# One limit and one guard per unit as sums over pairs: small softmax operations regrouped in a fused attention and gated feed-forward kernel

## The chip, the cores and the metric

One core of one Trainium2 chip. The metric is the device time of one execution in microseconds (us), given as the median of several runs. Engines are called by the profile's names: PE (TensorE, matrix products), PEld (its weight loads), DVE (VectorE), ACT (ScalarE), POOL (GpSimd) and SP (SyncE, which issues most DMAs).

## What is computed

```python
# q, k, v: (8 batches, 8 heads, 576, 64); tau = 0.02
scores = (1 / sqrt(64)) * q @ k^T
thresh = max(scores, axis=-1) - tau
scores = where(scores >= thresh, scores, -1e9)
attn = exp(scores - max(scores))
attn = attn / (sum(attn) + 1e-9)
x = (attn @ v), heads side by side                 # (8, 576, 512)

h = maximum(x @ w_in, 0)                           # w_in (512, 1024)
conv = three taps along the sequence, zero at both ends, weights (3, 1024)
out = (h * sigmoid(conv)) @ w_out                  # w_out (1024, 512)
```

All in float32. Each row of the softmax keeps only the scores within tau of the row's maximum.

## The kernel before

The work on attention is cut into 160 *units*: a pair of heads and one tile of 128 query rows, or, for the last 64 rows of a sequence, both heads in one tile of 128. For each batch the tiles form two *chunks* (rows 0 to 255 and 256 to 575), and after a chunk's units come its feed-forward products. In a unit, `unit(u, ...)`, each head goes through these steps; names in brackets are those that the profile shows:

1. PE computes the scores into a PSUM tile (`ps_s`, two buffers; L573 in batch 0, L580 after).
2. DVE takes each row's maximum with its sign turned (L588, into the small tile `few`).
3. ACT computes exp(score - maximum) into `em` (L597).
4. The *limit*, maximum minus tau, a column of 128 values, one operation for each head, on DVE, POOL or ACT (L594, L592).
5. The *mask* on DVE (L600): compare the scores with the limit, multiply with `em`, and sum the row into `few` at once.

For both heads together follow the *guard* (sum + 1e-9, L617, on DVE or POOL), its reciprocal (L624, DVE), and an operation for empty rows (L621, DVE or POOL: 1/576 where the sum is zero, else zero). Last comes the *norm* of each head, `em` x reciprocal + that column (L633, POOL in 287 of 288 cases). PE then turns `em` round (L692), ACT copies the result, and PE multiplies with v (L747, L756).

`mm1` computes one block of 128 hidden features for a chunk: PE (`ph`, L784), ReLU on ACT (L799) into `hp`, taps and gate on DVE (L806, L811), tanh on ACT (L813), and the split of the result into a high and a low part (L821 on ACT, L333 on POOL). `hp` has a column more at each end; where the chunk begins or ends a sequence POOL writes that column to zero each time (`edge`, L794 and L796). `mm2` is the last product (`po`, L842).

In the first stage DVE, POOL and ACT also split the feed-forward weights into two parts: 16 pieces of 512 columns (`stage`; L380 on POOL, L383, L386 and L389 on DVE, and L333 on POOL for four of the pieces), and 15 short DVE operations (L454) compute the ratios of the convolution's weights.

No loop sets the order in which an engine meets its operations. All steps are given to a `Plan` with a cost in nanoseconds, the tiles read and written, and other engines that may take them (`other`); a list scheduler plays through these costs and writes each engine's instructions in the order that comes out. A tile of a pool (`plan.buf`) becomes available when everything that used its buffer four (or three, two) turns before is done.

## Time and profile before

| what | value |
|---|---|
| median of 3 runs | 915.95 us (913.06 to 915.98) |
| span of the profiled execution | 910.8 us; no time of its own is given for it |
| PE busy | 874.6 us, 96% of the span |
| DVE busy | 751.2 us, 82% |
| ACT busy | 673.8 us, 74% |
| POOL busy | 603.5 us, 66% |
| L594 limits | 170 on DVE (mean 208 ns), 89 on POOL (351 ns); L592: 29 on ACT (287 ns) |
| L617 guards | 91 on POOL (296 ns), 69 on DVE (293 ns) |
| L621 empty rows | 93 on DVE (160 ns), 67 on POOL (245 ns) |
| L633 norms on POOL | 287, mean 924 ns |
| L794, L796 zero columns on POOL | 64 + 64, mean 96 and 97 ns |

The span runs from the first to the last instruction of one execution; the runs' times are some microseconds longer. A share of busy time is a mean over the whole span, in which the first stage (batch 0's attention and the weights) differs from the rest. "Idle before, releaser" in a group's row tells how long its engine waited just ahead of it, and for what.

### The profile page before, as it was taken

Reading aid. Unit: us, or ns where it says so; the run is one execution under the profiler, and the core shown is the slowest. Engines: PE = TensorE matmul, PEld = TensorE weight load, DVE = VectorE, ACT = ScalarE, POOL = GpSimd, SP = SyncE. Lnnn points to the kernel's source line nnn. Section 1 sums busy time; section 2 is a strip of 40 time slices with the busy share of each in tenths; the row PEclk is TensorE's granted clock in tenths of the full one; section 3 lists DMA queues with packets and bytes.
Section 4 is the critical chain, followed back from the end, with each engine's and each line's share of the span. In section 5 each row is a group of like instructions: output and inputs, shape, how many; then the busy total and the mean of one; then the engine's idle time right before and its main releaser. Section 6 shows DMA issues by size and latency. Waiting matters only on the chain.

```text
span 910.8 us, 19147 instructions
## 1 busy us (share of the span) xinstructions
PE 874.6 (96%) x6056; PEld 708.6 (78%) x6056; DVE 751.2 (82%) x1871; ACT 673.8 (74%) x1459; POOL 603.5 (66%) x1027
## 2 busy tenths in 40 slices
PE   5978799999999999999999999999999999999998
PEld 3545577878878788888788797887888878887896
DVE  5988999988988689987889789996988779997542
ACT  4878687878777777777768687877867778776642
POOL 2656778875767677685767767776776758675322
PEclk9989899999999999999999999999999999999999
DMA  6555257667764667647665377557667276654000
GB/s 213 155 162 170 57 143 197 149 178 181 198 175 113 163 175 198 158 116 202 169 157 157 117 201 191 140 118 202 173 176 179 89 187 159 181 137 112 13 24 35
DMA packets 148260, 137.02 MB, mean 150 GB/s; under 512 B 85312, under 2 KB 116288, under 8 KB 148160
## 3 DMA queue, kind: packets, MB, share of 16 engines
q1 hardware_dynamic: 147296, 133.90, 55.3%
q10 hardware_dynamic: 864, 1.90, 0.6%
q8 instruction: 49, 0.80, 0.4%
q14 instruction: 51, 0.42, 0.2%
HBM read 58.88 MB, written 25.95 MB: 93 GB/s over the span
## 4 chain that ended last, share of the span: by engine, by line
PE 73%; ACT 8%; DVE 6%; POOL 5%; DMA 4%; issue 3%; SPq 2%; ACTq 0%; POOLq 0%; DVEq 0%
PE po L842 20%; PE ph L784 16%; PE pa L756 12%; PE ps_s L580 11%; PE ps_t L692 9%; PE ps_s L573 3%; ACT em L597 2%; POOL em L633 2%; DVE em L600 2%; ACT eT L687 2%; PE pa L747 2%; DVE few L588 2%; DMA q<-in_qd_dram 1%; SPq L513 1%; DMA q<-q 1%
## 5 line engine op out<-in xcount | busy, mean ns | idle before, releaser
L633 POOL TENSOR_SCALAR em<-em,few 128x576 f32<-128x576 f32 x287 | 262.8, 924 | 29.9 <-DVE few L624 22.1
L600 DVE SCALAR_TENSOR_TENSOR em<-ps_s,few,em 128x576 f32<-128x576 f32 x288 | 230.5, 812 | 25.4 <-ACT em L597 17.1
L588 DVE TENSOR_REDUCE few<-ps_s 128x1 f32<-128x576 f32 x288 | 211.5, 748 | 39.3 <-PE ps_s L573 22.0
L597 ACT ACTIVATE em<-ps_s,few 128x576 f32<-128x576 f32 x288 | 210.5, 741 | 35.8 <-DVE few L588 31.5
L784 PE MATMUL ph<-x,w1h 128*128 128x322 f32 (+1 forms) x1024 | 233.7, 304 | 0.6 <-ACT hp L799 0.5
L687 ACT ACTIVATE eT<-ps_t 128x512 f32<-128x512 f32 (+2 forms) x360 | 168.0, 487 | 24.5 <-PE ps_t L692 22.4
L784 PEld LDWEIGHTS ph<-x,w1h 128*128 128x128 f32 x1024 | 173.1, 189 | 4.7 <-issue 3.0
L692 PE MATMUL ps_t<-ident,em 128*128 128x128 f32 x1060 | 157.8, 280 | 6.5 <-POOL em L633 5.1
L580 PE MATMUL ps_s<-ks,q 128*128 128x288 f32 x896 | 156.8, 306 | 5.3 <-DMA q<-q 2.1
L784 PE MATMUL ph<-x,w1l 128*128 128x322 f32 (+1 forms) x512 | 151.3, 295 | 0.0
L692 PEld LDWEIGHTS ps_t<-ident,em 128*128 128x128 f32 x1060 | 126.5, 143 | 31.5 <-POOL em L633 14.9
L580 PEld LDWEIGHTS ps_s<-ks,q 128*128 128x128 f32 x896 | 129.2, 189 | 20.2 <-issue 8.2
L333 POOL TENSOR_TENSOR gl<-t,gh 128x255 fp32r<-128x255 f32 (+9 forms) x192 | 119.6, 637 | 28.5 <-ACT gh L821 27.5
L756 PE MATMUL pa<-eT,v 128*64 128x320 f32 (+1 forms) x1024 | 132.1, 410 | 0.0
L842 PE MATMUL po<-w2h,gh 128*128 128x512 f32 x288 | 117.9, 409 | 0.3 <-ACT hp L799 0.3
L756 PEld LDWEIGHTS pa<-eT,v 128*64 128x64 f32 x1024 | 70.4, 137 | 59.3 <-issue 15.8
L842 PE MATMUL po<-w2l,gh 128*128 128x512 f32 x288 | 113.3, 393 | 0.0
L842 PE MATMUL po<-w2h,gl 128*128 128x512 f32 x288 | 113.1, 393 | 0.1
L806 DVE SCALAR_TENSOR_TENSOR t<-hp,cr 128x321 f32<-128x321 f32 (+1 forms) x128 | 75.6, 594 | 28.0 <-ACT hp L799 28.0
L784 PEld LDWEIGHTS ph<-x,w1l 128*128 128x128 f32 x512 | 96.8, 189 | 0.2
L813 ACT ACTIVATE t<-t,cm 128x321 f32<-128x321 f32 (+1 forms) x128 | 68.0, 535 | 25.2 <-DVE t L806 12.2
L811 DVE SCALAR_TENSOR_TENSOR t<-t,hp 128x321 f32<-128x321 f32 (+1 forms) x128 | 73.1, 573 | 11.4 <-ACT t L813 9.8
(80 smaller groups left out, 1104.1 us busy)
## 6 DMA issues: line engine op xcount, KB each, us to landing
q<-q SPq DMA_DIRECT2D x336, 64.0 KB, 2.1
v<-in_vc_dram SPq DMA_DIRECT2D x64, 288.0 KB, 3.8
rows<-parts SPq DMA_DIRECT2D x28, 576.0 KB, 3.3
k<-in_kp_dram SPq DMA_DIRECT2D x35, 320.0 KB, 3.5
out_dram<-ot SPq DMA_DIRECT2D x36, 256.0 KB, 2.3
xk<-in_kt_dram SPq DMA_DIRECT2D x28, 288.0 KB, 3.4
ks<-xk SPq DMA_DIRECT2D x56, 144.0 KB, 3.3
xq<-in_qt_dram SPq DMA_DIRECT2D x56, 128.0 KB, 2.9
```

Source lines behind the costliest of these rows:

```text
L333: engines[e].tensor_tensor(dst, x, y, op=ALU.subtract)
L580: nc.tensor.matmul(ps[:, c, :CH], lhsT=q[:, h, o:o + n], rhs=k[:, h, c * CH:(c + 1) * CH], start=(i == 0), stop=(i == 1))
L588: nc.vector.tensor_reduce(few[:rows, nm], ps[:rows, :, :CH], op=ALU.max, axis=mybir.AxisListType.XY, negate=True)
L597: nc.scalar.activation(view(), ps[:rows, :, :CH], AF.Exp, bias=few[:rows, nm])
L600: nc.vector.scalar_tensor_tensor(view(), ps[:rows, :, :CH], few[:rows, th], view(), op0=ALU.is_ge, op1=ALU.mult, accum_out=few[:rows, total])
L633: engines[e].tensor_scalar(sl, sl, by, to, op0=ALU.mult, op1=ALU.add)
L687: "act", act(w, True), lambda dst=dst, src=src: nc.scalar.activation(dst(), src(pt), AF.Copy),
L692: nc.tensor.transpose(out=pt[:, at:at + P], in_=em[:, int(b * P):int(b * P) + P], identity=ident[:])
L756: nc.tensor.matmul(pa[j * D:(j + 1) * D, :w], lhsT=vt[:, blk, :], rhs=eT[:, :w // D, blk, :], start=False, stop=(r == 3))
L784: nc.tensor.matmul(ph[:, :an], lhsT=w1[w][:, cb, fs], rhs=xs[cb][:, h, :an], start=(cb == 0 and i == 0), stop=(cb == NCB - 1 and i == 2))
L806: nc.vector.scalar_tensor_tensor(t[:, :kn], hp[:, k:kn + k], cr[:, j, f:f + 1], y, op0=ALU.mult, op1=ALU.add)
L842: nc.tensor.matmul(po[:], lhsT=x[:, f, at:at + P], rhs=w[:, f, :], start=(f == 0 and i == 0), stop=(f == NFB - 1 and i == 2))
```

## The change

Four small tiles `fews` and three `hps` are made once and stay; the buffers of `few` and `hp` now take them in turn (`home`) in place of pool tiles. What is constant in them is written once: tau in columns 1 and 3 of each `few`, 2^-80 x 576 in columns 5 and 7 (and in the rest until overwritten), and zero in the first and last column of each `hp`. With it:

- The limit is one operation for both heads, on DVE alone: a sum over the pairs (minus maximum, tau) with its sign turned. Both heads' masks come after it, so the first mask waits for the second head's maximum.
- The guard is a sum over the pairs (row sum, 2^-80 x 576), on DVE alone.
- There is no operation for empty rows. The norm is (em + 2^-80) x reciprocal, so that a row with no kept score comes out as 1/576. It has one per-row operand and a constant, and it may go to POOL or DVE, not to ACT.
- `edge` is gone; ReLU always writes from column 1, and the taps read from column o = 0 or 1.
- Costs in the plan differ: the norm on POOL 728 for 807, limits and guards 85, the tanh 92 more.

```diff
+    fews = [const(f"few{i}", [P, 12], F32) for i in range(FEW)]
+    hps = [const(f"hp{i}", [P, CW + 2], F32) for i in range(HPB)]
+    for x in fews:
+        op("pool", 100, lambda x=x: nc.gpsimd.memset(x[:], LEAST * S), w=[(x, 0)], ahead=200.0)
+        op(
+            "dve", 150, lambda x=x: nc.vector.tensor_scalar(x[:, 1:4:2], x[:, 1:4:2], 0.0, tau_sb[:], op0=ALU.mult, op1=ALU.add),
+            w=[(x, 0)], r=[(tau_sb, 0)], ahead=100.0
+        )
+    for x in hps:
+        op("pool", 100, lambda x=x: nc.gpsimd.memset(x[:, 0:CW + 2:CW + 1], 0.0), w=[(x, 0)], ahead=5.0)
...
-            def limit(e, nm=nm, th=th):
-                if e == "act":
-                    nc.scalar.activation(few[:rows, th], few[:rows, nm], AF.Identity, scale=-1.0, bias=ntau[:rows])
-                else:
-                    engines[e].tensor_scalar(few[:rows, th], few[:rows, nm], -1.0, ntau[:rows], op0=ALU.mult, op1=ALU.add)
+            def limit():
+                pairs = few[:rows, :2 * m].rearrange("p (h two) -> p h two", two=2)
+                nc.vector.tensor_reduce(few[:rows, 8:8 + m], pairs, negate=True, **add)
...
-            op("dve", 125, limit, w=[(few, ("th", h))], r=[(few, ("nm", h)), (ntau, 0)], ahead=a, other=[("pool", 260), ("act", 110)])
-            op("dve", 738, mask, w=[(em, h), (few, ("sum", h))], r=[(ps, 0), (few, ("th", h))], ahead=a)
+            late.append(mask)
+            if h == m - 1:
+                op("dve", 85, limit, w=[(few, "th")], r=[(few, ("nm", x)) for x in range(m)], ahead=a)
+        for h in range(m):
+            op("dve", 738, late[h], w=[(em, h), (few, ("sum", h))], r=[(pss[h], 0), (few, "th")], ahead=a)
...
-        def guard(e):
-            engines[e].tensor_scalar(few[:rows, inverse], few[:rows, sums], 1e-9, 1.0, op0=ALU.add, op1=ALU.mult)
-        def even(e):
-            engines[e].tensor_scalar(few[:rows, shift], few[:rows, sums], 0.0, 1.0 / S, op0=ALU.is_equal, op1=ALU.mult)
+        def guard():
+            pairs = few[:rows, 4:4 + 2 * m].rearrange("p (h two) -> p h two", two=2)
+            nc.vector.tensor_reduce(few[:rows, inverse], pairs, **add)
...
-                    engines[e].tensor_scalar(sl, sl, by, to, op0=ALU.mult, op1=ALU.add)
-            choice = {"pool": 807, "dve": 400, "act": 625}
+                engines[e].tensor_scalar(sl, sl, LEAST, few[:rows, 10 + h:11 + h], op0=ALU.add, op1=ALU.mult)
+            choice = {"pool": 728, "dve": 400}
...
-        def edge():
-            if o:
-                nc.gpsimd.memset(hp[:, 0:1], 0.0)
-            if k0 + kn == S:
-                nc.gpsimd.memset(hp[:, kn + 1:kn + 2], 0.0)
...
-        op("act", act(kn), lambda: nc.scalar.activation(t[:, :kn], t[:, :kn], AF.Tanh, scale=cm[:, 0, f:f + 1]), w=[(t, 0)], r=[(cr, 0)])
+        op("act", act(kn) + 92, lambda: nc.scalar.activation(t[:, :kn], t[:, :kn], AF.Tanh, scale=cm[:, 0, f:f + 1]), w=[(t, 0)], r=[(cr, 0)])
```

Since the scheduler sets the order, the whole program is ordered anew. Three places of it follow; the number at a name's end tells one use of a tile from another, and the line numbers of the changed kernel are L601 maximum, L605 limit, L611 mask, L632 guard, L635 reciprocal, L639 norm, L390 to L399 and L343 weight pieces.

First, DVE at the very start, where the first unit (`em_139` before, `em_145` now) runs. Before:

```order
L588 TENSOR_REDUCE few_132<-ps_s_0_123 128x1
L594 TENSOR_SCALAR few_132<-few_132,ntau 128x1
L588 TENSOR_REDUCE few_132<-ps_s_1_136 128x1
L600 SCALAR_TENSOR_TENSOR em_139,few_132<-ps_s_0_123,few_132,em_139 128x576
L600 SCALAR_TENSOR_TENSOR em_139,few_132<-ps_s_1_136,few_132,em_139 128x576
L588 TENSOR_REDUCE few_150<-ps_s_0_146 128x1
L624 RECIPROCAL few_132<-few_132 128x2
```

Now:

```order
L601 TENSOR_REDUCE few_77<-ps_s_0_131 128x1
L601 TENSOR_REDUCE few_77<-ps_s_1_147 128x1
L605 TENSOR_REDUCE few_77<-few_77 128x2
L611 SCALAR_TENSOR_TENSOR em_145,few_77<-ps_s_0_131,few_77,em_145 128x576
L611 SCALAR_TENSOR_TENSOR em_145,few_77<-ps_s_1_147,few_77,em_145 128x576
L601 TENSOR_REDUCE few_83<-ps_s_0_155 128x1
L632 TENSOR_REDUCE few_77<-few_77 128x2
L601 TENSOR_REDUCE few_83<-ps_s_1_159 128x1
L635 RECIPROCAL few_77<-few_77 128x2
```

The one limit stands between the second maximum and the first mask, with nothing beside it; the guard, which POOL did before, follows behind the next unit's first maximum.

Second, DVE in the second chunk of batch 0, in one unit (`em_863` before, `em_858` now) among the weight pieces. Before:

```order
L588 TENSOR_REDUCE few_849<-ps_s_0_838 128x1
L588 TENSOR_REDUCE few_849<-ps_s_1_844 128x1
L383 TENSOR_SCALAR stage_f<-stage_f 128x512
L600 SCALAR_TENSOR_TENSOR em_863,few_849<-ps_s_0_838,few_849,em_863 128x576
L386 SCALAR_TENSOR_TENSOR stage_f<-stage_712,stage_f 128x512
L600 SCALAR_TENSOR_TENSOR em_863,few_849<-ps_s_1_844,few_849,em_863 128x576
L389 SCALAR_TENSOR_TENSOR stage_f<-stage_712,stage_f 128x512
L621 TENSOR_SCALAR few_849<-few_849 128x2
L588 TENSOR_REDUCE few_900<-ps_s_0_883 128x1
```

Now:

```order
L601 TENSOR_REDUCE few_83<-ps_s_0_811 128x1
L601 TENSOR_REDUCE few_83<-ps_s_1_818 128x1
L605 TENSOR_REDUCE few_83<-few_83 128x2
L611 SCALAR_TENSOR_TENSOR em_858,few_83<-ps_s_0_811,few_83,em_858 128x576
L393 TENSOR_SCALAR stage_f<-stage_f 128x512
L611 SCALAR_TENSOR_TENSOR em_858,few_83<-ps_s_1_818,few_83,em_858 128x576
L396 SCALAR_TENSOR_TENSOR stage_f<-stage_763,stage_f 128x512
L632 TENSOR_REDUCE few_83<-few_83 128x2
L393 TENSOR_SCALAR stage_f<-stage_f 128x512
```

Both limits were POOL's here; the one that takes their place stands in DVE's line.

Third, POOL in the same stretch, with that unit's norm and the next one's. Before:

```order
L594 TENSOR_SCALAR few_849<-few_849,ntau 128x1 x2
L617 TENSOR_SCALAR few_849<-few_849 128x2
L380 TENSOR_SCALAR stage_f<-stage_f 128x512
L594 TENSOR_SCALAR few_900<-few_900,ntau 128x1
L633 TENSOR_SCALAR em_863<-em_863,few_849 128x576 x2
L594 TENSOR_SCALAR few_900<-few_900,ntau 128x1
L380 TENSOR_SCALAR stage_f<-stage_f 128x512
L617 TENSOR_SCALAR few_900<-few_900 128x2
L333 TENSOR_TENSOR w2l<-stage_f,w2h 128x512
L380 TENSOR_SCALAR stage_f<-stage_f 128x512
L633 TENSOR_SCALAR em_906<-em_906,few_900 128x576 x2
```

Now:

```order
L390 TENSOR_SCALAR stage_f<-stage_f 128x512 x2
L639 TENSOR_SCALAR em_858<-em_858,few_83 128x576
L343 TENSOR_TENSOR w2l<-stage_f,w2h 128x512
L639 TENSOR_SCALAR em_858<-em_858,few_83 128x576
L390 TENSOR_SCALAR stage_f<-stage_f 128x512
L343 TENSOR_TENSOR w2l<-stage_f,w2h 128x512
L390 TENSOR_SCALAR stage_f<-stage_f 128x512
L343 TENSOR_TENSOR w2l<-stage_f,w2h 128x512
L343 TENSOR_TENSOR gl<-t_0_929,gh 128x255
L639 TENSOR_SCALAR em_969<-em_969,few_85 128x576 x2
```

The four limits and two guards are gone from POOL's line; a unit's two norms now have a weight piece between them, and the next unit's come behind three of the four pieces that POOL subtracts.

More of the change, by code (lines that the diff above doesn't have):

```diff
@@ L21 @@
 HUGE = 3.0e38
+LEAST = 2.0 ** -80
+FEW = 4
 AHEAD = {'s': 6.25, 's4': 7.75, 't': 3.5, 'a': 3.5, 'prep': 4.25, 'w': 2.5, 'load': 7.75}
@@ L63, in __init__ @@
         self.pool, self.tag, self.bufs, self.shape, self.dtype, self.name = pool, tag, bufs, shape, dtype, name
-        self.tile, self.left = None, 0
+        self.tile, self.left, self.home = None, 0, None
     def __getitem__(self, key):
         if self.tile is None:
-            self.tile = self.pool.tile(self.shape, self.dtype, tag=self.tag, bufs=self.bufs, name=self.name)
+            self.tile = self.home or self.pool.tile(self.shape, self.dtype, tag=self.tag, bufs=self.bufs, name=self.name)
         return self.tile[key]
@@ L312, in tile_tau_attention_gated_ffn @@
     op("act", 450, lambda: nc.scalar.dma_start(tau_sb[:], tau.broadcast_to([P, 1])), w=[(tau_sb, 0)], ahead=205.0, late=2500)
-    ntau = const("ntau", [P, 1], F32)
-    op("dve", 70, lambda: nc.vector.tensor_scalar(ntau[:], tau_sb[:], -1.0, None, op0=ALU.mult), w=[(ntau, 0)], r=[(tau_sb, 0)], ahead=6.0)
+    fews = [const(f"few{i}", [P, 12], F32) for i in range(FEW)]
[8 more added lines that the diff above has]
+        op("pool", 100, lambda x=x: nc.gpsimd.memset(x[:, 0:CW + 2:CW + 1], 0.0), w=[(x, 0)], ahead=5.0)
     warm = const("warm", [P, 1], F32)
@@ L558, in unit @@
         em = plan.buf(wk, "em", EMS, [P, 2 * S], F32, f"em_{u}")
-        few = plan.buf(sm, "few", 4, [P, 10], F32, f"few_{u}")
+        few = plan.buf(sm, "few", FEW, [P, 12], F32, f"few_{u}")
+        few.home = fews[few.turn % FEW]
         a = AHEAD["s" if 2 * n > P else "s4"]
-        tiny = [("pool", 200)]
+        late, pss = [], []
+        add = dict(op=ALU.add, axis=mybir.AxisListType.X)
         for h, js in enumerate(heads):
             ps = plan.buf(ps_s, "ps_s", 2, [P, 2, 512], F32, f"ps_s_{u}_{h}")
-            nm, th, total = (slice(at + h, at + h + 1) for at in (0, 2, 4))
+            pss.append(ps)
+            nm, th, total = (slice(at, at + 1) for at in (2 * h, 8 + h, 4 + 2 * h))
             def mm(h=h, js=js, ps=ps):
@@ L608, in unit @@
             )
[L609 removed]
+            op("dve", 668, top, w=[(few, ("nm", h))], r=[(ps, 0), (few.home, 0)], ahead=a)
             op("act", 625, exp, w=[(em, h)], r=[(ps, 0), (few, ("nm", h))], ahead=a)
[L611 to L623 removed]
+            late.append(mask)
[3 more added lines that the diff above has]
+            op("dve", 738, late[h], w=[(em, h), (few, ("sum", h))], r=[(pss[h], 0), (few, "th")], ahead=a)
+        ss = [(few, ("sum", h)) for h in range(m)]
+        inverse = slice(10, 10 + m)
+        def guard():
+            pairs = few[:rows, 4:4 + 2 * m].rearrange("p (h two) -> p h two", two=2)
+            nc.vector.tensor_reduce(few[:rows, inverse], pairs, **add)
+        op("dve", 85, guard, w=[(few, "inverse")], r=ss, ahead=a)
         op("dve", 82, lambda: nc.vector.reciprocal(few[:rows, inverse], few[:rows, inverse]), w=[(few, "inverse")], ahead=a)
[L625 removed]
         for h in range(m):
@@ L638, in unit @@
             op(
-                home, choice[home], norm, w=[(em, h)], r=[(few, "inverse"), (few, "shift")], ahead=a, port=True,
+                home, choice[home], norm, w=[(em, h)], r=[(few, "inverse")], ahead=a, port=True,
                 other=[(e, ns) for e, ns in choice.items() if e != home]
```

24 lines of the change are left out of this document (8 added, 16 removed).

## The prediction

> **What bounds the kernel now.** I read the busy time of each engine stage by stage first (TensorE, PE, is busy 96% of the span on the page, which hides the difference between the stages), then what PE waits for, then the chain of work through the slow stretch, and last the prices of the small operations.
>
> ```profile
> 0.00:114.00 114.00, 90.43 (x518) 53.24 (x518) 94.14 (x225) 82.08 (x166) 65.67 (x108) 0.94 0.48 151
> 114.00:800.00 686.00, 677.23 (x4858) 565.09 (x4856) 592.74 (x1497) 531.86 (x1158) 491.19 (x828) 1.00 0.63 164
> ```
>
> The columns are the stretch, its length, then busy time of PE, PEld, DVE, ACT and POOL, granted clock, DMA share and GB/s. From 114 us on PE is the bound: 98.7% busy to 800 us, idle for 686.0 - 677.2 = 8.8 us. An operation taken off DVE, ACT or POOL there can be worth no more than that idle time. The first 114 us are another stage: PE is idle for 114.0 - 90.4 = 23.6 us, and DVE is the fullest engine (94.1 us, though its first limit starts only at 8.6). So the change is judged by the start. What PE waits for there, and the four stretches of 10 us that hold its two longest stalls (columns as before):
>
> ```profile
> PE ps_s L573 <- DVE em L600: 9.0, 4, 4.6
> PE ps_s L573 <- ACT q L503: 6.4, 1, 6.4
> PE ps_t L692 <- POOL em L633: 3.8, 6, 1.2
> PE ps_s L573 <- issue: 2.9, 1, 2.9
> ```
>
> ```profile
> 40.00:50.00 10.00, 7.35 (x49) 4.28 (x49) 8.74 (x32) 6.50 (x14) 4.21 (x9) 1.00 0.61 191
> 50.00:60.00 10.00, 7.86 (x26) 4.49 (x26) 7.99 (x20) 6.90 (x13) 4.41 (x7) 0.66 0.38 117
> ...
> 100.00:110.00 10.00, 5.07 (x36) 2.80 (x36) 9.91 (x22) 6.75 (x13) 6.11 (x9) 0.79 0.27 76
> 110.00:120.00 10.00, 9.99 (x63) 6.55 (x63) 8.81 (x24) 8.21 (x20) 6.53 (x12) 0.87 0.28 69
> ```
>
> The 6.4 us is the first load; no edit touches it. The 9.0 us are waits for a mask (L600), whose end frees a score tile. They and the 2.9 us lie mostly in two stalls: one of 4.6 us that ends at 52 us, where DVE computes the convolution's ratios, and one in two pieces, 2.0 and 2.9 us, between 101 and 108 us, where DVE is busy 9.91 of 10 us. After each the granted clock falls, to a mean of 0.66 in one stretch, and of 0.79 and 0.87 in two.
>
> **The change part by part.** First, POOL. Through the start the chain of work steps onto POOL's small operations seven times (0.19 to 0.79 us each); the list by line, the first with the crossing behind it, and the last three are:
>
> ```profile
> by line: issue 12.0%; DVE em L600 11.2%; PE ps_s L573 9.6%; POOL em L633 9.6%; DVE few L588 9.2%; ACT eT L687 4.2%; ACT em L597 4.2%; DVE stage_f L386 4.2%; PE ps_t L692 4.0%; DMA q<-in_qd_dram 3.8%; POOL stage_f L380 3.6%; DVE stage_f L389
> ...
> 65.54 0.56 POOL few L617
> 66.10 0.08 issue
> ...
> 86.56 0.42 POOL few L594
> ...
> 89.10 0.79 POOL few L594
> ...
> 90.83 0.30 POOL few L617
> ```
>
> All seven add up to 2.7 us. The changed kernel has no limit, guard or empty-row operation on POOL (its list there shows norms, weight pieces and the large subtractions alone), so I count -2.7, and -0.5 for seven crossings of some 0.08 us, since what takes their place stands in DVE's own line. Bounds: nothing, if another engine is as late at each of these places, and the whole that leaves POOL in the start, fifteen limits and fifteen guards by their medians, 15 x 0.265 + 15 x 0.301 = 8.5 us:
>
> ```profile
> L594 POOL TENSOR_SCALAR few<-few,ntau x15: 258/265/789, 9.8 to 89.1; 128x1 f32<-128x1 f32 x15
> L594 DVE TENSOR_SCALAR few<-few,ntau x11: 195/202/215, 8.6 to 110.7; 128x1 f32<-128x1 f32 x11
> L617 POOL TENSOR_SCALAR few<-few x15: 191/301/569, 11.5 to 113.2; 128x2 f32<-128x2 f32 x12, 128x1 f32<-128x1 f32 x3
> L617 DVE TENSOR_SCALAR few<-few x3: 142/155/169, 16.0 to 70.2; 128x2 f32<-128x2 f32 x2, 128x1 f32<-128x1 f32 x1
> L621 DVE TENSOR_SCALAR few<-few x13: 139/161/165, 16.1 to 113.4; 128x2 f32<-128x2 f32 x11, 128x1 f32<-128x1 f32 x2
> L624 DVE RECIPROCAL few<-few x18: 153/159/168, 12.7 to 113.8; 128x2 f32<-128x2 f32 x14, 128x1 f32<-128x1 f32 x4
> ```
>
> Second, the norm. It keeps its engine and size and exchanges one of two per-row operands for a number. No row has that form; the nearest are the norm itself and a POOL operation with two numbers on 512 columns:
>
> ```profile
> L633 POOL TENSOR_SCALAR em<-em,few x30: 816/827/1499, 13.0 to 109.5; 128x576 f32<-128x576 f32 x30
> L380 POOL TENSOR_SCALAR stage_f<-stage_f x16: 612/612/1006, 14.6 to 99.2; 128x512 f32<-128x512 f32 x16
> ```
>
> At 576 columns the second would be 612 x 576 / 512 = 689 ns. With one operand of each kind I take the middle, 758 ns, or 0.07 us less. The chain's list by line gives POOL's norm 9.6% of the start, 10.9 us or 13 norms, which makes -0.9 (bounds 0 and 13 x 0.138 = -1.8). In the steady part the same 0.07 us times 257 shortens an engine on which PE hardly waits.
>
> Third, what DVE takes over. Eighteen units (L624's count) lie in the start; their 18 limits, 18 guards and 18 reciprocals make 54 small operations, where DVE had 11 + 3 + 13 + 18 = 45 (six limits were on ACT). A row's duration isn't what it costs in DVE's line:
>
> ```profile
> 16.04 0.15 DVE L617 TENSOR_SCALAR few<-few 128x2 f32<-128x2 f32 x1
> 16.11 0.15 DVE L621 TENSOR_SCALAR few<-few 128x2 f32<-128x2 f32 x1
> 16.23 0.17 DVE L624 RECIPROCAL few<-few 128x2 f32<-128x2 f32 x1
> ```
>
> ```profile
> 306.80 1.42 DVE L588 TENSOR_REDUCE few<-ps_s 128x1 f32<-128x576 f32 x2 [3.83 <-PE ps_s L573]
> 308.26 0.21 DVE L594 TENSOR_SCALAR few<-few,ntau 128x1 f32<-128x1 f32 x1
> 308.44 0.82 DVE L600 SCALAR_TENSOR_TENSOR em<-ps_s,few,em 128x576 f32<-128x576 f32 x1
> ```
>
> Starts are 0.07 to 0.12 us apart where operations follow freely; I take 0.11. Where a limit stands directly between the maximum it needs and the mask that needs it, the step costs 0.30: two maxima that follow each other take 2 x 0.67 of the 1.64 us from the first's start to the mask's. A sum over pairs has no row; it is DVE work on two or four elements, nearest to the reciprocal of two, so I price it the same way. In the changed order 4 of the first 18 limits stand so, against two places before; the others have a weight piece or a reciprocal beside them. That makes 9 x 0.11 + 2 x 0.19 = +1.4. Bounds: all 18 limits at 0.30 and nothing cheaper elsewhere, 18 x 0.30 + 36 x 0.11 - (2 x 0.30 + 43 x 0.11) = +4.0; and, if every new one costs 0.07 and every old one 0.12, 54 x 0.07 - 45 x 0.12 = -1.6.
>
> Fourth, one limit for two heads: the first mask now waits for the second maximum, and the score tile behind it, with the next scores on PE, for that mask. In the order before, 118 of the 128 two-head units already run both maxima ahead of the first mask. Of the ten others four lie in the start, so at most 4 x 0.67 = 2.7 us, and nothing where DVE fills the time with weight pieces. I take +0.5.
>
> Fifth, DVE's weight operations stretch while POOL works on long ones:
>
> ```profile
> L389 DVE SCALAR_TENSOR_TENSOR stage_f<-stage,stage_f 128x512 uint32<-128x512 uint32 x16 | 13.8, 864 | 0.0
> ```
>
> ```profile
> L389 DVE SCALAR_TENSOR_TENSOR stage_f<-stage,stage_f x16: 674/690/1757, 23.2 to 103.5; 128x512 uint32<-128x512 uint32 x16
> ```
>
> The median is 0.690 us and the longest 1.757; the sixteen average 0.864, so 16 x 0.174 = 2.8 us of DVE's start go there. POOL's busy time in the start falls by the 8.5 us above and 30 x 0.07, a sixth of 65.7. I take the same share of the 2.8, -0.5 (bounds 0 and -2.8). [...]
>
> Sixth, the zero columns. The memsets (0.10 us each, 128 of them, six in the start) leave POOL's queue, where they waited for a tile that DVE still read and held the norms behind them. In the start POOL's chain holds none of them: 0. Seven small memsets and four setup operations on tau come ahead of the first maximum; the 6.4 us in which PE waits for its first load cover them.
>
> Seventh, the steady part. Of its 8.8 us of idle PE these name POOL's norm or DVE's softmax:
>
> ```profile
> PE ps_t L692 <- POOL em L633: 1.3, 3, 0.7
> PE ps_s L580 <- DVE em L600: 1.1, 2, 0.6
> PE ps_s L580 <- DVE few L594: 1.0, 2, 0.7
> ```
>
> That is 3.4 us; the order is planned anew and some waits return in other places, so I take a third, -1.2 (bounds -3.4, and +2 if as many new ones appear). PE's own work is the same list of products; the changes between kinds of products number 524 before and 526 after, counted in the order, and cost the same.
>
> The sum: -2.7 - 0.5 - 0.9 + 1.4 + 0.5 - 0.5 + 0 - 1.2 = -3.9 us. The span of 910.8 becomes 906.9. No separate time is given for the profiled execution; two of the three runs lie at 915.95 and 915.98, 5.15 us above the span, the third at 913.06, 2.3 above. I keep the median's distance: 912.0 us. The three runs differ by 0.3%, about what a measurement of this kernel can tell from no change, so 0.3% (2.7 us) is the bound of "same": 913.2 to 918.7.
>
> **The rivals.** One: the second stall goes as a whole. Behind its 4.9 us of idle PE the clock is missing 10 x 0.21 + 10 x 0.13 = 3.4 us of full speed. If the masks at 102 us come three microseconds earlier, PE has no gap long enough to lose its clock: -4.9 - 3.4 - 1.2 gives 906.4. For it: the chain from 86 to 100 us runs mostly over POOL, which loses 0.42 + 0.79 + 0.30 us of small work there. Against it: the four weight pieces that POOL subtracts itself remain, and DVE was without a gap. [...] Here the clock fell after two waits of 2.0 and 2.9 us.
>
> Two: nothing measurable. DVE paces the start and POOL's freed time is covered by it at each of the seven places. Then only +1.4 + 0.5 - 1.2 remain: 916.7. For it: DVE's work in the start doesn't shrink, and its limits and guards there were mostly on POOL already. Against it: POOL's pieces do stand in the chain.
>
> Three: slower. The new sums are dearer than a small operation, because each waits for its predecessor on DVE's own pipeline: at 0.30 for every limit the third term is +4.0, and at 0.30 for every guard too (18 x 0.19 more) +7.4. With DVE the pacer and nothing gained from POOL, +4.0 gives 920.0; it decides (over 918.7) from 0.23 us a limit on. For it: DVE is busy 94 of the 114 us, with its first limit at 8.6. Against it: 14 of the 18 limits have other work beside them. [...]
>
> **How the numbers follow.** The forecast (909 to 913.2) gets 0.36, the vanished stall (under 909) 0.20, no difference 0.27, slower 0.17. Faster is the sum of the first two, 0.56. The range leaves out the slower case and little of the low end: 904 (the stall's 906.4 less the steady part's other 2.2) to 918.7. The forecast's own range is 909 to 913.2: below it half of the room between 2.7 and 8.5 us of POOL, above it what reads as no difference.
>
> **What would show it.** In the changed profile: no POOL group on few apart from four memsets, and some 100 us less busy time there; a norm between 0.69 and 0.83 us; 160 limits and 160 guards on DVE with starts near 0.11 apart; PE idle of about 20 us in the first 114, and under 9 from there to 800. The stall at 48 us should remain, the one at 102 us should be shorter. The prediction is wrong if DVE's small operations hold it at over 0.2 us each, if the re-planned order opens a stall of its own after 114 us, or if the second stall's half clock vanishes.

## The result: 0.56% slower

| kernel | median of the runs, us | ratio to before, 95% interval |
|---|---|---|
| before | 915.81 (913.06 to 915.98) | |
| changed | 920.09 (918.24 to 921.62) | 1.0056 [1.0039, 1.0073] |

The forecast was 912.0, faster, in a range of 904 to 918.7. The time lies above the range, and at the number of rival three (920.0).

The profiled execution of the changed kernel has a span of 918.3 us in a time of 920.09, 1.8 us around the span, and in all runs on record it is 1.7 to 2.0. So the 910.8 us of the profile of before belong to a time of some 912.6 us (an estimate, 910.8 + 1.8), below all runs of the table, and not to the median. First the two stretches that the prediction set out from, of the changed kernel (columns as there):

```profile
0.00:114.00 114.00, 88.80 (x512) 53.16 (x513) 93.97 (x235) 78.61 (x155) 52.34 (x75) 0.95 0.46 151
114.00:800.00 686.00, 676.37 (x4807) 559.88 (x4807) 581.39 (x1459) 526.08 (x1127) 404.34 (x525) 1.00 0.64 164
```

PE did 88.8 us of work in the first 114 where it did 90.4 before: the start became worse by 1.6 us. In the second stretch it idles for 9.6 us, before 8.8. POOL lost what was foreseen (the page has 502.0 us for 603.5), and no engine is fuller than it was. The last of the start and what comes right behind it, in stretches of 10 us:

```profile
90.00:100.00 10.00, 8.04 (x53) 5.56 (x51) 8.09 (x15) 6.58 (x14) 7.35 (x8) 0.91 0.01 2
100.00:110.00 10.00, 6.50 (x48) 3.52 (x44) 7.95 (x20) 4.91 (x10) 5.35 (x6) 0.84 0.26 75
110.00:120.00 10.00, 7.63 (x39) 6.40 (x39) 7.83 (x19) 6.34 (x14) 5.69 (x7) 0.73 0.35 83
120.00:130.00 10.00, 9.18 (x51) 5.32 (x52) 8.16 (x20) 6.10 (x15) 4.05 (x5) 0.83 0.24 70
```

Before, PE was busy for 10.00, 5.07 and 9.99 of the 10 us in the first three of these rows. Now it has three stalls in four stretches (94 to 98, 104 to 110 and 116 to 122 us), with the granted clock below 1 from 90 to 130, and DVE isn't full in any of them. PE's longest waits from 90 to 126 us name ACT:

```profile
PE pa L753 <- ACT eT L693: 4.5, 3, 2.5
PE ph L791 <- ACT hp L800: 2.5, 1, 2.5
PE ps_s L586 <- DVE em L611: 0.7, 1, 0.7
```

Where the first of the three begins shows on POOL:

```profile
89.05 1.94 POOL L639 TENSOR_SCALAR em<-em,few 128x576 f32<-128x576 f32 x1 [1.79 <-DVE few L635]
90.96 1.28 POOL L343 TENSOR_TENSOR w2l<-stage_f,w2h 128x512 fp32r<-128x512 f32 x1
92.23 0.75 POOL L639 TENSOR_SCALAR em<-em,few 128x576 f32<-128x576 f32 x1
```

A weight piece stands between the two norms of one unit, so that the second head's norm starts 3.2 us after the first's, and PE's turning of `em`, ACT's copy and PE's product with v come behind it. The order before has the two norms in a row at this place. The first norm is also long here, 1.94 us for a median of 0.75. That the new order makes these stalls is likely, and these rows alone don't show it.

How far PE came by 200 us, and in the 600 us behind that, before and then in the changed kernel:

```profile
0.00:200.00 200.00, 174.30 (x1111) 121.60 (x1113) 174.63 (x428) 152.98 (x321) 133.07 (x220) 0.97 0.54 155
200.00:800.00 600.00, 593.36 (x4269) 496.73 (x4261) 512.24 (x1294) 460.96 (x1003) 423.79 (x715) 1.00 0.64 165
```

```profile
0.00:200.00 200.00, 171.03 (x1059) 118.23 (x1060) 169.00 (x418) 144.64 (x296) 103.80 (x143) 0.96 0.52 152
200.00:800.00 600.00, 594.14 (x4260) 494.81 (x4259) 506.35 (x1275) 460.06 (x987) 352.88 (x456) 1.00 0.65 165
```

By 200 us PE has worked through 52 products fewer (1059 for 1111; scores 276 for 304, and of no kind more). From there to 800 us it does as many as before (4260 for 4269). So, in these two single runs, the changed kernel loses its time in the start.

The new operations themselves, each line's durations (least, median, longest) over the whole program:

```profile
L605 DVE TENSOR_REDUCE few<-few x160: 131/150/159, 9.6 to 851.9; 128x2 f32<-128x4 f32 x128, 128x1 f32<-128x2 f32 x32
...
L632 DVE TENSOR_REDUCE few<-few x160: 132/148/158, 12.9 to 853.8; 128x2 f32<-128x4 f32 x128, 128x1 f32<-128x2 f32 x32
...
L639 POOL TENSOR_SCALAR em<-em,few x288: 735/747/1942, 14.1 to 855.1; 128x576 f32<-128x576 f32 x144
```

A limit or guard lasts 0.15 us and never more than 0.16, a norm 747 ns in the median. None of them is dear by its row. What the limit costs is seen in the distances of starts. A unit of the changed kernel in which nothing else is at hand, on DVE:

```profile
265.55 1.41 DVE L601 TENSOR_REDUCE few<-ps_s 128x1 f32<-128x576 f32 x2
267.00 0.16 DVE L605 TENSOR_REDUCE few<-few 128x2 f32<-128x4 f32 x1
267.26 0.82 DVE L611 SCALAR_TENSOR_TENSOR em<-ps_s,few,em 128x576 f32<-128x576 f32 x1
```

From the second maximum's start a limit behind it starts 782 ns later (median of 55 such places in the whole trace), where an operation that doesn't need the maximum, a tap of the convolution, starts after 664 (45 places). The mask starts 262 ns after the limit that it needs; an operation that doesn't need it starts after 67. So a joint limit between maximum and mask costs 118 + 262 = 380 ns, where one with other work beside it costs 67. Of 160 limits 55 stand between both, 26 more directly ahead of their mask.

### The profile page after: what moved, and what is told of

The parts are those of the page before. It is cut to its first block, busy times and chain, and to the rows that moved or that the text cites. A ratio compares the mean times of both kernels' runs of the same rounds, so it can differ in the third digit from the quotient of the medians.

```text
span 918.3 us, 18671 instructions
## 1 busy us (share of the span) xinstructions
PE 879.0 (96%) x6056; PEld 708.3 (77%) x6056; DVE 747.0 (81%) x1862; ACT 670.9 (73%) x1429; POOL 502.0 (55%) x660
## 4 chain that ended last, share of the span: by engine, by line
PE 71%; DVE 10%; ACT 5%; DMA 4%; issue 4%; POOL 3%; SPq 1%; ACTq 0%; POOLq 0%; DVEq 0%
PE po L842 18%; PE ph L791 15%; PE pa L762 12%; PE ps_s L593 11%; PE ps_t L698 9%; PE ps_s L586 3%; DVE few L601 3%; DVE em L611 3%; POOL em L639 2%; PE pa L753 2%; DMA q<-q 2%; DVE t L806 2%; ACT em L608 1%; ACT eT L693 1%; DMA xk<-in_kt_dram 1%
## 5 line engine op out<-in xcount | busy, mean ns | idle before, releaser
L639 POOL TENSOR_SCALAR em<-em,few 128x576 f32<-128x576 f32 x288 | 239.3, 841 | 178.7 <-DVE few L635 168.6
L611 DVE SCALAR_TENSOR_TENSOR em<-ps_s,few,em 128x576 f32<-128x576 f32 x288 | 226.0, 812 | 20.6 <-ACT em L608 12.6
L608 ACT ACTIVATE em<-ps_s,few 128x576 f32<-128x576 f32 x288 | 208.1, 741 | 47.3 <-DVE few L601 44.4
L791 PE MATMUL ph<-x,w1h 128*128 128x322 f32 (+1 forms) x1024 | 238.6, 305 | 4.1 <-ACT hp L800 3.5
L601 DVE TENSOR_REDUCE few<-ps_s 128x1 f32<-128x576 f32 x288 | 209.5, 748 | 36.4 <-PE ps_s L586 20.1
L343 POOL TENSOR_TENSOR gl<-t,gh 128x255 fp32r<-128x255 f32 (+9 forms) x192 | 121.2, 645 | 140.2 <-ACT gh L821 137.8
L593 PE MATMUL ps_s<-ks,q 128*128 128x288 f32 x896 | 153.2, 303 | 3.8 <-DMA q<-q 1.7
L762 PE MATMUL pa<-eT,v 128*64 128x320 f32 (+1 forms) x1024 | 136.7, 419 | 0.0
L806 DVE SCALAR_TENSOR_TENSOR t<-hp,cr 128x321 f32<-128x321 f32 (+1 forms) x128 | 82.9, 649 | 33.1 <-ACT hp L800 30.7
L806 DVE SCALAR_TENSOR_TENSOR t<-hp,cr,t 128x321 f32<-128x321 f32 (+1 forms) x128 | 82.8, 651 | 0.6
```

The lines of the kernel that those rows point to most:

```text
L343: engines[e].tensor_tensor(dst, x, y, op=ALU.subtract)
L593: nc.tensor.matmul(ps[:, c, :CH], lhsT=q[:, h, o:o + n], rhs=k[:, h, c * CH:(c + 1) * CH], start=(i == 0), stop=(i == 1))
L601: nc.vector.tensor_reduce(few[:rows, nm], ps[:rows, :, :CH], op=ALU.max, axis=mybir.AxisListType.XY, negate=True)
L608: nc.scalar.activation(view(), ps[:rows, :, :CH], AF.Exp, bias=few[:rows, nm])
L611: nc.vector.scalar_tensor_tensor(view(), ps[:rows, :, :CH], few[:rows, th], view(), op0=ALU.is_ge, op1=ALU.mult, accum_out=few[:rows, total])
L639: engines[e].tensor_scalar(sl, sl, LEAST, few[:rows, 10 + h:11 + h], op0=ALU.add, op1=ALU.mult)
```

## The experiments

Two theories came out of this. Operations: the joint limit costs the time, by where it stands on DVE. Order: the newly planned order costs it, with its stalls between 94 and 122 us. All ratios are to the kernel before, timed on the same chip among the same runs; its medians in the four sets were 915.79, 914.86, 912.98 and 913.97 us, so the ratios are compared and not the times.

### Operations and order apart

The first two kernels cross the two: all new operations, written out in the order of the kernel before, and the old operations (two scalar limits, guard, empty-row operation and two-operand norm, all small ones on DVE) in the order of the changed kernel.

```diff
 # first kernel: before's plan, where DVE has reached a mask whose limit is missing
+                if len(tops) == m and not have:
+                    limits(0, m)          # one sum over both pairs
 # second kernel: the changed plan
             def limit():
+                for i in range(m):
+                    nc.vector.tensor_scalar(few[:rows, 2 + i:3 + i], few[:rows, i:i + 1], -1.0, ntau[:rows], ...)
```

> The changed kernel's operations in the order of the kernel before: TensorE's list is the same row for row, limits and guards are sums over pairs on DVE (170 limits, since in ten units the first mask still runs ahead of the second maximum), no empty-row operation, the one-operand norm on POOL, zero columns written once. Theory 'order' (the operations are no dearer, the new order opens stalls of PE in the first 125 us): 909 to 914 us, no new stall between 94 and 122 us. Rival 'dear sums' (the new small operations hold DVE up): 918 to 921 us, as the changed kernel.

Measured: 920.51 us, ratio 1.0063 [1.0046, 1.0079]. The operations alone, in the old order, lose as much as the whole change. The theory of the order as the only cause falls.

> The other half of the table: the changed kernel's order, row for row on TensorE, with the old operations in it (two limits of their own in place of the joint one, guard and empty-row operation as tensor-scalar operations, all on DVE; the two-operand norm; the zero column written by POOL each time). Theory 'order': 919 to 925 us, as slow as the changed kernel or slower, with stalls of PE at 94 to 122 us. Rival 'dear sums': 913 to 917 us, since the sums are gone.

Measured: 933.61 us, ratio 1.0197 [1.0178, 1.0217]. Both theories missed. The new order is far worse with the old operations in it, so the two don't add up, and within the new order the new operations are the better ones. Its norms average 940 ns for the changed kernel's 841, its guards 244 for 149; how much of the loss each brings was not told apart.

Two more kernels change the tanh's price in the plan alone, from one's to the other's. The operations are the same, but in the first of the two 14 small ones move from DVE to POOL with the new plan (1857 and 1041 instructions for 1871 and 1027).

```diff
-        op("act", act(kn), ... AF.Tanh ...)
+        op("act", act(kn) + 92, ... AF.Tanh ...)      # in the kernel before; the reverse in the changed one
```

> The kernel before with one number of the plan changed, the tanh priced 92 ns higher; every instruction is the same, only the order differs. Theory 'order': the time moves by some us either way (911 to 921), with PE's idle time and its half-clock stretches in the first 130 us. Rival 'dear sums': 915.8, within 0.3%.

> The changed kernel with the tanh priced as before; same instructions, another order. Theory 'order': another draw between 909 and 921, below the changed kernel if its order was an unlucky one. Rival 'dear sums': 920, within 0.3% of the changed kernel.

Measured: before with the new price 917.25, ratio 1.0026 [1.0011, 1.0041]; changed with the old price 922.65, ratio 1.0086 [1.0065, 1.0107]. The new price costs the one kernel 0.26% and gives the other 0.3% (there the intervals, [1.0065, 1.0107] and the changed kernel's [1.0039, 1.0073], overlap). It isn't the cause, but it tells what another plan of the same work is worth: some 0.3%, of either sign.

### Which operation

Still in the order of the kernel before, the limits were split from the rest of the change.

```diff
 # third kernel: everything new but the limits
+                    engines[e].tensor_scalar(few[:rows, th], few[:rows, nm], -1.0, ntau[:rows], ...)   # a head's, on its old engine
 # fourth kernel: only the limits new; guard, empty rows, norm and zero columns as before
```

> The whole change except the limits, in the order of the kernel before: a limit for each head as a scalar operation on the engine it had (DVE, POOL or ACT), with the guard as a sum over pairs, no empty-row operation, the norm with one operand per row and the zero columns written once. Theory L (the joint limit on DVE is what costs the time, by the waits before and behind it): the kernel that had all new operations in this order ran at 920.5 us; without the joint limit 911 to 916. Rival R (the guard as a sum, or lasting tiles, cost as much): 918 to 921.

> The opposite: in the order of the kernel before only the limits are new (one sum over pairs for both heads on DVE where the order allows it), with the old guard, empty-row operation, norm and zero columns. Theory L: 918 to 922, idle PE between 130 and 800 us at 12 us or more against 8.6. Rival R: 914 to 917.

Measured: without the joint limit 914.36, ratio 1.0002 [0.9990, 1.0014]; with nothing but it 920.66, ratio 1.0071 [1.0058, 1.0085]. The joint limit is the whole loss in this order. The other side of it: guard as a sum, shorter norm, no empty-row operation and no zero columns, 79 us less of POOL's time (524.5 for 603.5), are worth nothing that can be measured.

The same edit with the order planned anew: the changed kernel with a scalar limit for each head, POOL and ACT as alternatives.

> The changed kernel with the limits alone as before (one scalar operation a head, POOL and ACT as alternatives), and the order planned anew from there. Theory L: 911 to 916. Theory O: the plan sets the time, 917 to 923, or where the new plan happens to have no stalls of its own in the start, about that of the first kernel of this set.

Measured: 915.28, ratio 1.0002 [0.9984, 1.0020]. Here too the loss is gone with the joint limit, though the order changed with it.

### What about it: waits, form, or one for two

In the changed kernel, every instruction in its place, the waits were taken away: the limit sums constants and the mask compares with a constant.

```diff
-                pairs = few[:rows, :2 * m]...
+                pairs = still[:rows, :2 * m]...
-                    view(), ps[:rows, :, :CH], few[:rows, th], view(), ...
+                    view(), ps[:rows, :, :CH], still[:rows, 0:1], view(), ...
```

> The changed kernel with every instruction in its place, but the limit sums over a tile of constants and the mask compares with a constant, so that neither waits for the maximum in front of it (the weights are then not those of the reference). Theory L: the step from a maximum over limit to mask falls from some 0.38 to about 0.1 us, and the time from 920 to 912 to 916. Theory O (the planned order of the start, with its stalls between 94 and 122 us, costs the time; the waits are hidden): 918 to 921, with those stalls still there.

Measured: 917.68, ratio 1.0036 [1.0023, 1.0050]. Between the two: a good third of the loss went, and the stalls after 94 us are still there (7.99, 6.28 and 7.00 us of PE in the three stretches from 90 to 120).

Next the form. The joint limit in its place, as one scalar operation on both heads' columns:

```diff
-                nc.vector.tensor_reduce(few[:rows, 8:8 + m], pairs, negate=True, **add)
+                nc.vector.tensor_scalar(few[:rows, 8:8 + m], few[:rows, 0:2 * m:2], -1.0, ntau[:rows], op0=ALU.mult, op1=ALU.add)
```

> The changed kernel, every instruction in its place, with the joint limit written as one scalar operation on both heads' maxima (DVE) in place of the sum over pairs. Theory F (the form of the limit costs the time: a sum waits longer for the maximum in front of it and holds the mask longer, 262 ns against 178 to 189): some 80 limits in front of their mask take 0.07 to 0.1 us less each, 6 to 8 us of DVE, and the time falls from 920 to 915 to 918. Theory J (being one limit for two heads, late and on DVE, costs it, in either form): 918.5 to 921.5.

Measured: 937.07, ratio 1.0262 [1.0238, 1.0287]. Both theories missed, by 16 us and more. The groups of DVE, this kernel's limits for two heads and for one:

```profile
L605 DVE TENSOR_SCALAR few<-few,ntau 128x2 f32<-128x2 f32 x128 | 65.2, 509 | 2.0
...
L605 DVE TENSOR_SCALAR few<-few,ntau 128x1 f32<-128x1 f32 x32 | 5.9, 204 | 0.0
```

and over all 160, least, median and longest:

```profile
L605 DVE TENSOR_SCALAR few<-few,ntau x160: 186/255/1419, 9.9 to 868.9; 128x2 f32<-128x2 f32 x128, 128x1 f32<-128x1 f32 x32
```

Two elements take 509 ns, one takes 204. In the trace, the limits that start while POOL is in an operation of over 0.4 us have a median of 642 ns, the others 218 (682 and 222 for those on two elements). The sum over pairs of the changed kernel shows no such split: 149 and 151 ns. So this scalar operation on two elements waits for POOL's operation, and a sum over two pairs doesn't. The scalar guards on DVE of the kernel before wait too, from 130 to 800 us with a mean of 364 ns for a median of 170:

```profile
L617 DVE TENSOR_SCALAR few<-few 128x2 f32<-128x2 f32 x46 | 16.7, 364 | 0.9
```

In the whole trace 18 of them start when such a POOL operation has over 200 ns left, and each ends 23 to 61 ns behind it; 85 joint sums of the changed kernel start so, and none lasts over 159 ns. The operation for empty rows of the kernel before, scalar and on two elements, has 157 ns beside such a POOL operation and 158 without (medians), but 35 of the 37 beside one start in its last 136 ns. The other two take 298 and 467 ns and end 27 and 26 ns behind it.

Then "one for two" was undone: in the order of the kernel before, with all new operations, a sum over one pair for each head at the place of its old limit, all 288 on DVE.

```diff
             def limit(e, h=h):
-                if h == m - 1 and len(tops) == m and not have:
-                    limits(0, m)
+                limits(h, 1)
...
```

> All new operations in the order of the kernel before, but one sum over a pair for each head, at the place where the kernel before computed that head's limit; all on DVE (288 of them, where the joint version has 170). Theory J: the first mask no longer waits for the second maximum, so 913 to 917 against 920.5 for the joint version. Theory F, or the mere move of the limits from POOL and ACT to DVE: 919 to 923, with more DVE time than the joint version.

Measured: 915.05, ratio 1.0019 [1.0003, 1.0034], against 1.0063 [1.0046, 1.0079] with joint limits in the same order. With 118 limits more on DVE it is faster, so neither the sum's form nor the move to DVE is the main cause; the 0.19% that is left may be theirs. One unit in both, first with the joint limit:

```profile
266.24 0.76 DVE L613 TENSOR_REDUCE few<-ps_s 128x1 f32<-128x576 f32 x1
266.92 0.15 DVE L648 TENSOR_REDUCE few<-few 128x2 f32<-128x4 f32 x1
267.10 0.17 DVE L654 RECIPROCAL few<-few 128x2 f32<-128x2 f32 x1
267.23 0.76 DVE L613 TENSOR_REDUCE few<-ps_s 128x1 f32<-128x576 f32 x1
268.02 0.16 DVE L585 TENSOR_REDUCE few<-few 128x2 f32<-128x4 f32 x1
268.29 0.82 DVE L630 SCALAR_TENSOR_TENSOR em<-ps_s,few,em 128x576 f32<-128x576 f32 x1
...
269.77 0.62 DVE L828 SCALAR_TENSOR_TENSOR t<-hp,cr 128x321 f32<-128x321 f32 x1
```

and with a limit for each head:

```profile
264.24 0.76 DVE L613 TENSOR_REDUCE few<-ps_s 128x1 f32<-128x576 f32 x1
264.91 0.14 DVE L641 TENSOR_REDUCE few<-few 128x2 f32<-128x4 f32 x1
265.09 0.17 DVE L647 RECIPROCAL few<-few 128x2 f32<-128x2 f32 x1
265.18 0.13 DVE L585 TENSOR_REDUCE few<-few 128x1 f32<-128x2 f32 x1
265.28 0.76 DVE L613 TENSOR_REDUCE few<-ps_s 128x1 f32<-128x576 f32 x1
266.01 0.82 DVE L623 SCALAR_TENSOR_TENSOR em<-ps_s,few,em 128x576 f32<-128x576 f32 x1
266.75 0.08 DVE L623 DVE_READ_ACCUMULATOR em<-ps_s,few,em 128x1 f32 x1
266.75 0.15 DVE L585 TENSOR_REDUCE few<-few 128x1 f32<-128x2 f32 x1
...
267.75 0.63 DVE L821 SCALAR_TENSOR_TENSOR t<-hp,cr 128x321 f32<-128x321 f32 x1
```

From the first maximum to the operation behind the second mask both take DVE 3.5 us (269.77 - 266.24 and 267.75 - 264.24). But the first mask starts 2.05 us after the first maximum with a joint limit and 1.77 with two: the second limit is done behind the first mask. Over the whole trace the limits take DVE 44 us in both kernels, from start to next start. What differs is the place: the first mask follows the last maximum with no limit between them in 56 units of this kernel, and in 6 of the joint one, where 88 joint limits stand there instead. The mask frees the score tile that PE needs next. PE's waits for it from 114 to 800 us, joint and then single:

```profile
PE ps_s L605 <- DVE em L630: 3.1, 8, 0.5
...
PE ps_s L598 <- DVE em L630: 0.9, 2, 0.6
```

```profile
PE ps_s L605 <- DVE em L623: 1.4, 4, 0.5
...
PE ps_s L598 <- DVE em L623: 0.7, 1, 0.7
```

These waits differ by 1.9 us only. But PE's list is the same in both kernels, row for row, so its steps can be compared one by one. From its 500th product to its 5500th PE takes 716.2 us with joint limits and 709.6 with single ones. Of the 6.5 us between them 6.2 lie in the 179 steps that lead from another product to a score product, from start to start. So the loss arises where PE needs a free score tile. (These are two single runs, 7.2 us apart in time; the ratios are some 4 us apart.) It arises all along the program and not in the start: with joint limits in this order PE has as many products by 200 us as the kernel before (1113 for 1111), and fewer from there to 800 (4206 for 4269).

```profile
0.00:200.00 200.00, 173.25 (x1113) 120.49 (x1113) 177.16 (x442) 150.90 (x309) 106.97 (x149) 0.97 0.54 155
200.00:800.00 600.00, 589.51 (x4206) 490.67 (x4201) 506.70 (x1264) 453.73 (x975) 344.80 (x451) 1.00 0.63 164
```

Then the waits alone, in the order of the changed kernel kept word for word: two sums in the place of one, first head first.

```diff
-                pairs = few[:rows, :2 * m].rearrange("p (h two) -> p h two", two=2)
-                nc.vector.tensor_reduce(few[:rows, 8:8 + m], pairs, negate=True, **add)
+                for i in range(m):
+                    pair = few[:rows, 2 * i:2 * i + 2].rearrange("p (h two) -> p h two", two=2)
+                    nc.vector.tensor_reduce(few[:rows, 8 + i:9 + i], pair, negate=True, **add)
```

> The changed kernel with its order kept word for word; the joint sum is replaced, in its place, by two sums over one pair, first head first. Two instructions stand where one stood, but the first doesn't need the maximum in front of it, and the first mask doesn't need the second. Theory W: the step from the last maximum over the limits to the first mask shrinks from 0.38 to some 0.2 to 0.25 us, and the time falls to 917 to 919, as with masks that wait for nothing (917.7). Theory S: 920 to 923.

Measured: 918.40, ratio 1.0040 [1.0026, 1.0054]. The unit shown above, in this kernel:

```profile
262.97 1.41 DVE L601 TENSOR_REDUCE few<-ps_s 128x1 f32<-128x576 f32 x2
264.30 0.27 DVE L606 TENSOR_REDUCE few<-few 128x1 f32<-128x2 f32 x2
264.55 0.82 DVE L612 SCALAR_TENSOR_TENSOR em<-ps_s,few,em 128x576 f32<-128x576 f32 x1
```

From the maxima's start to the mask 1.58 us, with one joint sum 1.71: two instructions are 0.13 us shorter than one, since the first needs the maximum before last and the mask needs the sum before last (in the changed kernel 67 ns from a limit to an operation that doesn't need it, and 262 to one that does). In time it is 0.16% less than the changed kernel, as with the free masks (0.20%); the intervals of the three overlap, so this share of the loss is likely rather than proven.

Last, the price: the changed kernel planned with 340 ns for a limit instead of 85.

> The changed kernel with the same instructions, planned with a price of 340 ns for the limit in place of 85. If the plan's wrong price is what lets limits stand directly between their maximum and their mask, fewer stand so and the time is 913 to 918; if the place costs nothing or the plan can't avoid it, 918 to 923.

Measured: 917.37, ratio 1.0041 [1.0022, 1.0060]. With 40 limits between maximum and mask for 55 it lies in the expected range, and no surer than the other two.

### A way that fails and a way that wins

No limit at all: the mask compares the exponentials with exp(-tau) and reads no scores.

```diff
-                    view(), ps[:rows, :, :CH], few[:rows, th], view(), op0=ALU.is_ge, ...
+                    view(), view(), etau[:rows], view(), op0=ALU.is_ge, ...
```

> The changed kernel without any limit: the mask compares the exponentials with exp(-tau), so it reads no score tile and waits for no limit; the score tile is free after the exponential. Theory L: DVE loses 128 limits and their waits, PE's waits for a mask before the next scores vanish: 904 to 913. Rival: the mask, with two inputs from SBUF in place of one from PSUM, stretches beside POOL by 0.1 us or more each, as the taps of the convolution do: 914 to 922.

Measured: 947.10, ratio 1.0369 [1.0342, 1.0396]; the rival named the cause, and missed the size by 25 us. The mask, whose row in the changed kernel has a mean of 812 ns, here:

```profile
L603 DVE SCALAR_TENSOR_TENSOR em<-em,etau 128x576 f32<-128x576 f32 x288 | 282.5, 995 | 29.6 <-ACT em L600 27.7
```

Its median is 820, its longest 1971 ns. The masks that start while POOL is in an operation of over 0.4 us have a median of 1203 ns, the others 814; in the changed kernel, where the scores come from PSUM, it is 811 and 814. The norms on POOL are stretched in turn (991 ns for 841 in the mean).

What the runs pointed to was the whole change with a limit for each head, as a sum over one pair right behind its maximum, planned anew, with the new and with the old tanh price:

```diff
+            def limit(h=h):
+                pair = few[:rows, 2 * h:2 * h + 2].rearrange("p (h two) -> p h two", two=2)
+                nc.vector.tensor_reduce(few[:rows, 8 + h:9 + h], pair, negate=True, **add)
...
+            op("dve", 85, limit, w=[(few, ("th", h))], r=[(few, ("nm", h))], ahead=a)
+            op("dve", 738, mask, w=[(em, h), (few, ("sum", h))], r=[(ps, 0), (few, ("th", h))], ahead=a)
```

> The whole change except that each head has its own limit, a sum over one pair priced like the joint one, right after its own maximum; the order is planned anew. Theory W (what costs the time is that the joint sum stands between the last maximum and the first mask and waits for both on DVE): 911 to 916, since a head's sum has the other head's maximum beside it. Theory S (the mere number of limits that DVE has taken from POOL and ACT): 919 to 923, with 128 more operations on DVE than the changed kernel.

> The kernel with a sum for each head, with the tanh priced as before the change, planned anew: the same instructions in another order. If the plan's order alone moves the time by a few tenths of a per cent either way, as the two kernels with the other tanh price did, this differs from the first kernel of this set by up to 4 us; otherwise within 1 us. Either may come out under the kernel before (909 to 917).

Measured: 910.17, ratio 0.9969 [0.9950, 0.9987], and 912.64, ratio 0.9970 [0.9952, 0.9988]. Both are faster than the kernel before by 0.3%, and than the changed one by 0.9%, in two different orders. Put together, three plans with the joint limit (the changed kernel, the one with the old tanh price, and the one with 340 ns for a limit) have ratios of 1.0041 to 1.0086, and three plans without it (the one with scalar limits and these two) 0.9969 to 1.0002. The first of the two, in the stretches of the result's first fence:

```profile
0.00:114.00 114.00, 91.01 (x537) 53.70 (x537) 98.23 (x259) 82.98 (x167) 53.88 (x78) 0.99 0.48 154
114.00:800.00 686.00, 677.23 (x4868) 564.19 (x4869) 592.79 (x1586) 527.30 (x1133) 402.35 (x530) 1.00 0.64 165
```

DVE has more to do than in the changed kernel (98.2 us for 94.0 in the start), PE 2.2 us more done at 114 us, and the clock stands at 0.99 for 0.95. From 90 to 130 us:

```profile
90.00:100.00 10.00, 10.00 (x83) 7.55 (x82) 10.00 (x16) 7.86 (x19) 8.45 (x8) 1.00 0.27 74
100.00:110.00 10.00, 6.55 (x43) 4.32 (x41) 9.53 (x24) 5.20 (x11) 8.72 (x9) 0.87 0.35 85
110.00:120.00 10.00, 9.06 (x65) 6.29 (x63) 9.29 (x25) 8.37 (x21) 4.73 (x7) 0.96 0.18 53
120.00:130.00 10.00, 10.00 (x63) 8.28 (x60) 9.17 (x27) 9.90 (x23) 6.54 (x8) 1.00 0.52 135
```

One stall is left where the changed kernel had three.

## Why the prediction was wrong

**The new order in the start.** One step that failed is a term that isn't in the sum: stalls that the newly planned order opens in the start. The prediction says that "the one at 102 us should be shorter" and allows for new waits in the steady part alone ("+2 if as many new ones appear"), though it judges the change by the start. The runs show three stalls from 94 to 122 us in its place, 52 products fewer at 200 us, and hardly anything lost from there to 800 us (4260 products for 4269).

**The third term, and rival three's price for it.** The other step that failed is "a sum over pairs has no row; ... so I price it the same way", together with the count of four limits between maximum and mask in the first 18. By its own distance to the next start a sum is even cheaper than the 0.11 us taken (0.067). But a limit between maximum and mask is 0.38 and not 0.30, and there are 55 of them in the program, with 26 more directly ahead of a mask. I counted the start alone and gave the steady part no price for them. In the order of the kernel before the loss arises there (4206 products for 4269 from 200 to 800 us); in the changed order what these waits cost arises in the start: without them PE has 1079 products at 200 us, with two sums in place 1074, for 1059, and from there to 800 us 4265 and 4256 for 4260. Rival three, "each waits for its predecessor on DVE's own pipeline", named what the distances show, 262 ns to a mask that needs the limit and 67 to an operation that doesn't; that DVE's pipeline is behind it, no run shows. That its 920.0 agrees with 920.09 is partly chance: its sum had 18 limits of the start at 0.30, +4.0 in all, and no stalls of a new order, while taking those waits away gave back 0.16 to 0.20%, 1.5 to 1.8 us.

**The fourth term.** "118 of the 128 two-head units already run both maxima ahead of the first mask" is true, and the wrong question. What the joint limit moved ahead of the first mask wasn't the second maximum but the limit itself: with single limits the first mask can follow the second maximum at once. The term was +0.5 us; in the old order, joint limits against single ones measure 0.44%, 4 us.

**The first, second and fifth terms: POOL.** Their premise held (POOL has 101.5 us less, the norm's median is 747 ns for the 758 taken), their worth didn't. In the old order the guard, the empty-row operation, the norm and the zero columns together give 1.0002. With the limits off POOL as well, its chain of seven small operations is gone, and the ratio is 1.0019. What stood in the chain of waits was no more than the last of several things that were about equally late: the first term's lower bound said so, "another engine is as late at each of these places", and rival two was built on it. Only together with a new order and single limits does something come of it, 0.3%.

**The sixth term**, zero columns for nothing, is in the same 1.0002 and stands.

**The seventh term** took a gain of 1.2 us from the steady part; PE's idle time there grew by 0.8. And "if the re-planned order opens a stall of its own after 114 us" came true a little earlier, from 94 us on. The stall at 48 us got shorter (PE is busy 7.30 and 9.29 us in the stretches from 40 and 50 us, for 7.35 and 7.86), and where one stood at 102 us there are three from 94 to 122.

**The distance of time and span.** The 5.15 us around the span were wrong, 1.7 to 2.0 is what all runs show. It changes no sign; it shows that the sum was made against a run of some 912.6 us, shorter than the three runs of the kernel before.

Open stays the rest of the loss in the changed order, 0.36 to 0.40%, when the waits on DVE are gone. Three stalls of that order are seen in the profile, and three orders planned without the joint limit come out 0.3 to 0.7% better than that. That all three plans with it are slower than all three without speaks for the tie between two heads forcing a worse order on the scheduler; that this one fell out badly within the 0.3% that another plan is worth is not excluded.

## What to carry to other kernels

Before joining two small operations into one, ask what stands between the last input and the first user: one operation for both halves sits on the way of the first half, and its two waits (0.118 and 0.262 us here) are paid there, while two halves fill each other's waits. Where the order is planned anew, look at the order for stalls of its own before adding up terms. An operation's price in a plan is the distance to the next start, in the place where it will stand; the duration in its row tells neither, and a count made in one stage doesn't hold for the program. A small scalar operation whose mean is far above its median (364 ns against 170 for the old guard) may be waiting for another engine, and another form of it may not have to (the sum: 149 ns beside POOL's operation, 151 without).

## What was not expected of the hardware

- The scalar limit on DVE on two float32 elements a row in SBUF waits for POOL's operation (median 682 ns beside one of over 0.4 us against 222, longest 1419); on one element it does not (206 ns beside such an operation and 213 without, in the kernel before), and a sum over two pairs doesn't (149 and 151). The old scalar guard on two elements waits as well: of 18 that start with over 200 ns of such an operation left, each ends 23 to 61 ns behind it.
- On DVE, a limit that needs the long maximum in front of it starts 782 ns after it, a tap that doesn't need it 664; behind a joint limit a mask that needs it starts after 262 ns, an operation that doesn't after 67, and a reciprocal starts 191 ns after the guard that it needs (medians in the changed kernel).
- A mask with both inputs in SBUF takes 1203 ns in the median beside a POOL operation of over 0.4 us and 814 without one; with the scores in PSUM it is 811 and 814.
